# Linear attention into a feed-forward layer: reciprocals at the head of a period, quotients one period later

## The chip, the core and the metric

The kernel runs on one core of a Trainium2 chip. Its engines run side by side, each through its own instructions in order: TensorE (PE: matmuls; PEld: its weight loads), VectorE (DVE), ScalarE (ACT), GpSimd (POOL) and SyncE (SP), which here issues nearly all DMA transfers. The metric is the device time of one execution in microseconds (us), lower is better, given as the median of several runs.

## The reference

```python
def phi(x):
    proj = np.einsum('bhsd,df->bhsf', x, w_phi)
    proj = proj - np.max(np.abs(proj), axis=-1, keepdims=True)
    return np.concatenate([np.exp(proj), np.exp(-proj)], axis=-1)
q_p, k_p = phi(q), phi(k)                      # q, k, v: 8 x 8 x 576 x 64
kv = np.einsum('bhsf,bhsd->bhfd', k_p, v)
z = np.sum(k_p, axis=2)
num = np.einsum('bhsf,bhfd->bhsd', q_p, kv)
den = np.einsum('bhsf,bhf->bhs', q_p, z)[..., None] + 1e-06
x = (num / den)                                # rows put together: 4608 x 512
h = x @ w_in                                   # 512 x 2048, handed over in 8-byte floats
g = h - np.tanh(h)
out = g @ w_out                                # 2048 x 512, 8-byte floats
```

## The kernel before

**Attention.** Two heads form a unit; there are 32. `period(i)` is called for i = 0 to 32 and writes out by hand the order of everything; no scheduler reorders it. A period does one step for each of several units: `a` = unit i is projected in three rounds (`project`, line 214; each followed on VectorE by `less_max`: the maximum, line 224, and the subtraction, line 231, which frees the PSUM tile for the next round), and its key exponentials are taken; `c` = unit i-1 gets its K-V product (`kv`, line 274) and its transposed query side; `p` = unit i-2 gets numerator (`num`, line 319, copied to `d`) and denominator (`denom`, line 334).

For `r` = unit i-3 the denominator is copied to `dd` (line 349) and loaded, spread over 128 partitions, as `dn` (line 354). In the middle of the same period, behind the second round, comes `den_recip` (reciprocal `rn`, line 362, written to a row `rr` in DRAM, line 363) and `den_spread` (`rr` read back to 64 partitions for each head, `rb`, line 370). For `r2` = unit i-4, one period on, `den_mul` (line 375) multiplies `d` by `rb` on VectorE, and `x_store` (line 378) writes the result to DRAM (`xs`).

Each period also decodes one 128-row or 128-column block of w_in (even) or w_out (odd) from 8-byte floats: `dec_load` (lines 156 and 161, tile `raw`, two buffers), `dec_0` on ScalarE (line 168) and `dec_1` to `dec_3` on VectorE (lines 172 to 180). `split_w` splits decoded blocks into a rounded high part and a low part (POOL, line 97); fourteen of the 32 are split in attention, eighteen "late" ones in the first feed-forward group. `behind` (line 187) is a one-column copy that keeps POOL behind a VectorE instruction. The Q/K tile (576 KB, line 196) is loaded two periods ahead and V (320 KB, line 200) at the start of its own period, each into the buffer of two units before.

**Feed-forward.** Twelve groups of 384 rows, each in sixteen steps: `stage1` (lines 534 to 556: twelve matmuls, then ScalarE and VectorE work), `split_g` (`gh` on ScalarE, line 562; `gl` on POOL, line 563) and `stage2` (lines 569 to 572). Stage 2 trails stage 1 by two steps. Here a scheduler orders instructions, but those under `pin` keep program order. The last units' reciprocals and quotients (POOL's) and the late splits are put into the first group's steps.

Of the kernel before, what the change touches and what calls it, by code (L numbers as in the profile page):

```python
# [8 lines left out]
F32 = mybir.dt.float32  # L9
# [5 lines left out]
BF16 = mybir.dt.bfloat16  # L15
# [4 lines left out]
P = 128  # L20
# [12 lines left out]
def tile_linear_attention_moe(  # L33
# [10 lines left out]
    nc = tc.nc  # L44
    B, H, S, D = dims
# [11 lines left out]
    AHEAD = 7  # L57
    PC = 2 * S
    NCT = DM // P
    NF = DFF // P  # L60
# [61 lines left out]
    with ExitStack() as c1:  # L122
# [6 lines left out]
        ps_c = c1.enter_context(tc.tile_pool(name="ps_c", bufs=1, space=PSUM))  # L129
        ps_d = c1.enter_context(tc.tile_pool(name="ps_d", bufs=3, space=PSUM))  # L130

        zt = p1.tile([P, 256], BF16, name="zt")
        nc.gpsimd.memset(zt, 0.0)


        pw = ps_d.tile([P, 512], F32, tag="po", name="warm")

# [12 lines left out]
        def dec_load(n):  # L150
            u = Dec()
            u.nm = f"{'io'[n % 2]}{n // 2}"
            u.f, u.d = n // 2, (wi, wo)[n % 2]
            u.r = raw.tile([P, DM], U64, tag="raw", name=f"raw{u.nm}")
            if n % 2 == 0:
                nc.sync.dma_start(
                    u.r.rearrange("p (c f) -> p c f", f=P),
                    w_in[:, u.f * P : (u.f + 1) * P].rearrange("(c p) f -> p c f", p=P),
                )
            else:  # L160
                nc.sync.dma_start(u.r, w_out[u.f * P : (u.f + 1) * P, :])
            return u
# [7 lines left out]
        def dec_1(u):  # L170
            a = u.a
            nc.vector.tensor_scalar(f32(a), f32(a), CMIN, CMAX, ALU.max, ALU.min)
            nc.vector.tensor_scalar(a, a, 3, None, ALU.logical_shift_left)
# [4 lines left out]
        def dec_3(u):  # L178
            w = wpool.tile([P, DM], F32, tag="w", name=f"w{u.nm}")
            nc.vector.scalar_tensor_tensor(  # L180
                w.bitcast(U32), u.hi, 0x80000000, u.a, ALU.bitwise_and, ALU.bitwise_or
            )
            u.d[u.f] = w


        def behind(x):
            nc.gpsimd.tensor_copy(mark, f32(x[:, 0:1]))
# [10 lines left out]
        def load_v(u):  # L198
            u.v = p2.tile([P, 5, 2, D], F32, tag="v", name=f"v{u.i}")
            nc.sync.dma_start(u.v.rearrange("p j e d -> p (j e d)"), v5[u.i])  # L200
# [139 lines left out]
                        )  # L340

        def num_copy(u):
            u.d = tail.tile([P, S], F32, tag="d", name=f"d{u.i}", bufs=3)
            for c in range(2):
                nc.scalar.copy(u.d[:, c * CH : (c + 1) * CH], u.po[c][:, 0:CH])

        def denom_copy(u):
            u.dd = tail.tile([P, CH], F32, tag="dd", name=f"dd{u.i}", bufs=2)
            nc.scalar.add(u.dd, u.pd[:, 0:CH], 1e-6)

        def den_recip_load(u):
# [5 lines left out]
        def den_recip(u, pin=lambda ins: ins):  # L357
            dn = u.dn
            rr = dr.tile([2, S], F32, tag="rr", name=f"rr{u.i}")
            w = 2 * S // P  # L360
            rn = tail.tile([P, w], F32, tag="rn", name=f"rn{u.i}", bufs=4)
            pin(nc.vector.reciprocal(rn, dn))
            nc.sync.dma_start(rr.rearrange("a s -> (a s)").rearrange("(p c) -> p c", c=w), rn)
            u.rr, u.rn = rr, rn

        def den_spread(u):
            rr = u.rr
            rb = tail.tile([P, S], F32, tag="rb", name=f"rb{u.i}", bufs=2)
            for e in range(2):
                nc.sync.dma_start(rb[e * D : (e + 1) * D, :], rr[e : e + 1, :].broadcast_to([D, S]))  # L370
            u.rb = rb

        def den_mul(u, eng=nc.vector, pin=lambda ins: ins):
            x = u.rb
            pin(eng.tensor_tensor(x, u.d, x, ALU.mult))  # L375

        def x_store(u):
            nc.sync.dma_start(xs[u.b // 2][u.hp, :, (u.b % 2) * S : (u.b % 2 + 1) * S], u.rb)
# [16 lines left out]
        def unit(i):  # L395
            return units[i] if 0 <= i < NU else None
# [14 lines left out]
        lows = []  # L411

        def period(i):
            a, c, p, r, r2 = (unit(i - n) for n in range(5))
            w = dec[i - 2] if 2 <= i < NU + 2 else None
            last = i == NU
            if a:
                a.kp = kpb[i % 2]
                if i == 0:
                    warm(16)  # L420
                project(a, 0)
                less_max(a, 0)
            if r:
                denom_copy(r)
                den_recip_load(r)
            if 3 <= i <= NU:
                dec.append(dec_load(i - 1))
            if 1 <= i < NU:
                load_v(a)
            if p:  # L430
                ksum_copy(p)
            if w:
                if i == 2:
                    dec_0(w)
                dec_1(w)
            if r2:
                den_mul(r2)
                x_store(r2)
            n = i - 3
            if 0 <= n < 4 * AHEAD and n % 2 == 0:  # L440
                lows.extend(split_w(n // 2))
            if c:
                k_exp(c, 2)
                if w:
                    behind(r2.rb if r2 else w.a)
                kadd(c, (4,))
            if 0 <= n < 4 * AHEAD:
                lows.pop(0)()
            if p:
                num(p)  # L450
                num_copy(p)
            if last:
                for j in range(NCT):
                    x_split(xt[0], j)
            if i < 2:
                warm(8 + 26 * i)
            if a:
                project(a, 1, (ps_tr, "tr") if i == 0 else None)
                less_max(a, 1)
                k_exp(a, 0)  # L460
            if r:
                den_recip(r)
                den_spread(r)
            if w:
                dec_2(w)
                dec_3(w)
                behind(w.d[w.f])
            if c:
                kv(c)
                kv_copy(c)  # L470
            if last:
                ksum(c, ps_d, "po")
                ksum_copy(c)
            if a:
                k_exp(a, 1)
                kadd(a, (2, 3))
            if 2 <= i < NU:
                dec_0(dec[i - 1])
            if a:
                project(a, 2, (ps_d, "po") if i == 0 else None)  # L480
                less_max(a, 2)
            if i + 2 < NU:
                load(units[i + 2])
            if c:
                turn(([(p, "s")] if p else []) + [(c, "k")] + ([(c, "s")] if last else []))
                q_side(c)
            if p:
                denom(p)
            if c and not last:
                ksum(c)  # L490
            if last:
                num(c)
                num_copy(c)
                dec_0(dec[i - 1])
                denom_copy(p)
                den_recip_load(p)
                w = dec[NU - 1]
                dec_1(w)
                dec_2(w)
                dec_3(w)  # L500
                denom(c)
                denom_copy(c)
                den_recip_load(c)
            if i == NU - 6:
                xt[0] = x_tiles(0)
            if 0 <= i - (NU - 6) < NCT:
                x_load(0, xt[0], i - (NU - 6))
# [6 lines left out]
    with ExitStack() as c2:  # L514
# [73 lines left out]
        for i in range(len(steps) + 2):  # L588
            if i < len(steps):
                g, f = steps[i]  # L590
                if f == 0:
                    po[g] = [ps_o.tile([P, DM], F32, tag="o", name=f"po{g}_{t}") for t in range(G)]
                gs[i] = stage1(g, f, *xt[g][:2])
                if g + 1 < NG:
                    if f == 0:
                        xt[g + 1] = x_tiles(g + 1)
                    if f % 3 == 0 and f < 3 * NCT:
                        x_load(g + 1, xt[g + 1], f // 3)
                    if f % 3 == 2 and f < 3 * NCT:
                        x_split(xt[g + 1], f // 3, pin)  # L600
            if 1 <= i <= len(steps):
                g, f = steps[i - 1]
                gg[i - 1] = split_g(g, f, gs.pop(i - 1), G)
            if 1 <= i <= 2:
                den_recip(units[i - 3], pin)
                den_spread(units[i - 3])
            if 2 <= i <= 4:
                den_mul(units[i - 5], nc.gpsimd, pin)
                x_store(units[i - 5])
            while late and late[0] <= 2 * AHEAD + i * NL // (NF - 1):  # L610
                split_w(late.pop(0), pin)[0]()
            if i >= 2:
                g, f = steps[i - 2]
                stage2(po[g], f, *gg.pop(i - 2), G)
                if f == NF - 1:
                    store(g * G, po.pop(g), G)
# [55 lines left out]
```

## Time and profile before

| | |
|---|---|
| median of 3 runs | 1168.69 us (1167.58 to 1170.34) |
| the profiled execution | 1172.38 us, its span 1170.6 |
| busy, share of the span | PE 97%, VectorE 74%, ScalarE 71%, POOL 36% |
| attention | about the first 356 us |
| DMA share, attention from 33.65 to 344.96 us | 0.61, 190 GB/s |
| DMA share, 450 us to the end | 0.07, 22 GB/s |

A row of the timeline gives start, duration, engine, line, operation, output and input; in brackets, how long the engine idled before it and what ended that. `SPq` rows are DMA issues on SyncE's queue, not transfers. "To landing" is from an issue to its data in place. In the list of waits stand total, number and longest.

### The profile page before, as it was taken

The page shows a single profiled execution, that of the slowest core. Times are in us where ns is not written, and L with a number is a line of the kernel's source. Part 1 is how long each engine was busy: PE and PEld are TensorE (multiplying, and loading weights), DVE is VectorE, ACT ScalarE, POOL GpSimd, SP SyncE. Part 2 cuts the span into 40 slices and gives each one's busy share as a digit, 9 for nine tenths or more (in the row PEclk, how much of TensorE's full clock was granted, in tenths as well). Part 3 has the DMA queues.
Part 4 walks back from the last instruction along what each step waited for, and adds up shares of the span by engine and source line. Part 5 has one row for each costly group of instructions (what it writes and reads, how often), then busy time and mean ns, then how long its engine had stood idle before and what let it go on. Part 6 is the DMA issues. An engine that isn't in the chain of part 4 may idle for free.

```text
span 1170.6 us, 21022 instructions
## 1 busy us (share of the span) xinstructions
PE 1137.5 (97%) x7578; PEld 951.9 (81%) x7578; DVE 863.3 (74%) x1429; ACT 833.4 (71%) x1908; POOL 417.3 (36%) x441
## 2 busy tenths in 40 slices
PE   8998999999899999999999999999999999999998
PEld 6666666666568889999999999999999999999996
DVE  5788688788777877677777767777777767777665
ACT  4876877788678766676766667676676667676665
POOL 3565466465545742222222222222222222222222
PEclk9999999999999999999999999999999999999999
DMA  4556565666652000010000000010101001000000
GB/s 153 158 185 199 174 195 195 210 194 187 203 170 81 31 29 21 8 41 14 34 21 34 15 21 28 15 41 14 35 15 34 21 8 41 14 28 1 28 1 28
DMA packets 51177, 85.61 MB, mean 73 GB/s; under 512 B 13313, under 2 KB 28033, under 8 KB 51073
## 3 DMA queue, kind: packets, MB, share of 16 engines
q1 hardware_dynamic: 50912, 84.20, 22.8%
q8 instruction: 60, 0.98, 0.4%
q14 instruction: 45, 0.36, 0.1%
q10 hardware_dynamic: 160, 0.07, 0.0%
HBM read 65.08 MB, written 19.02 MB: 72 GB/s over the span
## 4 chain that ended last, share of the span: by engine, by line
PE 78%; DMA 11%; DVE 5%; ACT 2%; issue 2%; POOL 1%; SPq 1%; DVEq 0%; ACTq 0%; POOLq 0%
PE ph L534 33%; PE po L572 11%; PE po L570 11%; PE po L569 11%; DMA rb<-rr 5%; DMA rr<-rn 3%; PE pp L214 3%; PE po L319 2%; DVE m L224 2%; DMA rawo<-in_moe_w_out 2%; PE pd L334 2%; PE pc L274 1%; PE ptt L241 1%; DVE t L231 1%; DVE rb L375 1%
## 5 line engine op out<-in xcount | busy, mean ns | idle before, releaser
L563 POOL TENSOR_TENSOR gl<-s,gh 128x384 fp32r<-128x384 f32 x192 | 196.0, 1021 | 568.7 <-ACT gh L562 567.5
L541 ACT ACTIVATE y<-ph 128x384 f32<-128x384 f32 x192 | 94.5, 492 | 238.1 <-PE ph L534 238.1
L534 PE MATMUL ph<-xh,wli 128*128 128x384 f32 x768 | 259.1, 337 | 0.8 <-POOL wli L97 0.8
L534 PE MATMUL ph<-xh,whi 128*128 128x384 f32 x768 | 258.7, 337 | 0.0
L534 PE MATMUL ph<-xl,whi 128*128 128x384 f32 x768 | 257.9, 336 | 0.0
L550 DVE SCALAR_TENSOR_TENSOR s<-s,y 128x384 f32<-128x384 f32 x192 | 110.9, 577 | 174.3 <-ACT s L543 174.2
L569 PE MATMUL po<-who,gh 128*128 128x512 f32 x576 | 227.1, 394 | 1.6 <-ACT gh L562 1.6
L570 PE MATMUL po<-wlo,gh 128*128 128x512 f32 x576 | 226.8, 394 | 0.0
L572 PE MATMUL po<-who,gl 128*128 128x512 f32 x576 | 164.3, 393 | 1.3 <-POOL gl L563 1.3
L534 PEld LDWEIGHTS ph<-xh,whi 128*128 128x128 f32 x768 | 144.3, 188 | 8.9 <-issue 0.5
L534 PEld LDWEIGHTS ph<-xl,whi 128*128 128x128 f32 x768 | 144.1, 188 | 8.2
L534 PEld LDWEIGHTS ph<-xh,wli 128*128 128x128 f32 x768 | 144.0, 188 | 1.2 <-POOL wli L97 1.2
L556 DVE COPY_PREDICATED s<-mk,th 128x384 f32<-128x384 uint32 x176 | 123.7, 703 | 18.9 <-DVE th L555 0.9
L572 PEld LDWEIGHTS po<-who,gl 128*128 128x128 f32 x576 | 107.9, 188 | 27.6 <-POOL gl L563 2.9
L224 DVE TENSOR_REDUCE m<-pp 128x4 f32<-128x512 f32 (+3 forms) x98 | 91.8, 939 | 49.9 <-PE pp L214 48.7
L283 POOL TENSOR_TENSOR ss<-ss,kp 128x512 f32<-128x512 f32 x96 | 122.7, 1278 | 9.4 <-ACT kp L268 4.4
L569 PEld LDWEIGHTS po<-who,gh 128*128 128x128 f32 x576 | 107.8, 187 | 20.2 <-ACT gh L562 3.3
L570 PEld LDWEIGHTS po<-wlo,gh 128*128 128x128 f32 x576 | 108.2, 188 | 16.3
L268 ACT ACTIVATE kp<-t 128x256 f32<-128x256 f32 (+2 forms) x256 | 108.4, 481 | 17.6 <-DVE t L231 16.4
L543 ACT ACTIVATE s<-y,bias_t 128x384 f32<-128x384 f32 x192 | 118.4, 617 | 3.3 <-POOL gl L563 3.3
L549 ACT ACTIVATE mk<-y,bias_t 128x384 f32<-128x384 f32 x192 | 117.7, 613 | 0.5 <-DVE s L556 0.5
L214 PEld LDWEIGHTS pp<-wph,qk 64*128 64x128 f32 x1152 | 74.0, 190 | 49.6 <-issue 19.0
(353 smaller groups left out, 1744.6 us busy)
## 6 DMA issues: line engine op xcount, KB each, us to landing
qk<-in_qkT SPq DMA_DIRECT2D x31, 576.0 KB, 4.9
v<-in_v SPq DMA_DIRECT2D x32, 320.0 KB, 5.3
rb<-rr SPq DMA_DIRECT2D x64, 144.0 KB, 3.4
xs<-rb SPq DMA_DIRECT2D x32, 288.0 KB, 3.9
x<-xs SPq DMA_DIRECT2D x48, 192.0 KB, 2.4
out<-o SPq DMA_DIRECT2D x36, 256.0 KB, 2.3
rawi<-in_moe_w_in SPq DMA_DIRECT2D x16, 512.0 KB
rawo<-in_moe_w_out SPq DMA_DIRECT2D x16, 512.0 KB
```

Source lines behind the costliest of these rows:

```text
L214: nc.tensor.matmul(heads[e][:, o * F : (o + 1) * F], u.qk[hs, j * P : (j + 1) * P], wph[hs, :], start=True, stop=True)
L224: nc.vector.tensor_reduce(m[:, e], x, AX.X, ALU.max, apply_absolute_value=True)
L283: nc.gpsimd.tensor_tensor(u.ss, u.ss, u.kp[:, :, j], ALU.add)
L534: nc.tensor.matmul(h, wt[:, c * P : (c + 1) * P], x[:, c, 0:N], start=(i == 0), stop=(i == 3 * NCT - 1))
L543: nc.scalar.activation(s1, y, AF.Square, bias=bias_t[:, 0:1])
L549: nc.scalar.activation(mk, y, AF.Relu, bias=bias_t[:, 2:3])
L550: nc.vector.scalar_tensor_tensor(s1, s1, PC1, y, ALU.add, ALU.mult)
L556: nc.vector.copy_predicated(gs, mk.bitcast(U32), hh)
L563: pin(nc.gpsimd.tensor_tensor(gl, gs, f32(gh), ALU.subtract))
L569: nc.tensor.matmul(po[t], a, wo[f][0], start=(f == 0), stop=False)
L570: nc.tensor.matmul(po[t], a, wo[f][1], start=False, stop=False)
L572: nc.tensor.matmul(po[t], gl[:, t * P : (t + 1) * P], wo[f][0], start=False, stop=(f == NF - 1))
```

## The change

- The reciprocal of a unit moves from the middle of period u+3 to the head of period u+4, ahead of the first round. Its quotient and store move from period u+4 to u+5 (`r3`), at the same place in the period. The spread follows the store of the unit before it.
- `d` has four buffers in place of three; `dd` one in place of two.
- V is loaded one period earlier, behind the spread; its buffer's last reader is the K-V product of the same period. A weight block is loaded behind `dec_3`, the last reader of its buffer, and so about half a period earlier.
- At the end three units are left for reciprocals (steps 5, 7, 9 of the first group; before, two in steps 1 and 2) and four for quotients (6, 8, 10, 12; before, three in 2 to 4). The late splits run in steps 2 to 14 (0 to 15 before).
- The matmuls that keep TensorE busy at the start read the identity in place of a zero tile, which is no longer written.

```diff
-        zt = p1.tile([P, 256], BF16, name="zt")
-        nc.gpsimd.memset(zt, 0.0)
+        zt = ident.bitcast(BF16)
...
-            u.d = tail.tile([P, S], F32, tag="d", name=f"d{u.i}", bufs=3)
+            u.d = tail.tile([P, S], F32, tag="d", name=f"d{u.i}", bufs=4)
...
-            u.dd = tail.tile([P, CH], F32, tag="dd", name=f"dd{u.i}", bufs=2)
+            u.dd = tail.tile([P, CH], F32, tag="dd", name=f"dd{u.i}", bufs=1)
...
-            a, c, p, r, r2 = (unit(i - n) for n in range(5))
+            a, c, p, r, r2, r3 = (unit(i - n) for n in range(6))
...
+            if r2:
+                den_recip(r2)
             if a:
...
-            if 3 <= i <= NU:
-                dec.append(dec_load(i - 1))
-            if 1 <= i < NU:
-                load_v(a)
...
+            if r3:
+                den_mul(r3)
+                x_store(r3)
             if r2:
-                den_mul(r2)
-                x_store(r2)
+                den_spread(r2)
+            if i + 1 < NU:
+                load_v(units[i + 1])
...
-                    behind(r2.rb if r2 else w.a)
+                    behind(r3.rb if r3 else w.a)
...
-            if r:
-                den_recip(r)
-                den_spread(r)
             if w:
                 dec_2(w)
                 dec_3(w)
+                if i < NU:
+                    dec.append(dec_load(i))
...
-            if 1 <= i <= 2:
-                den_recip(units[i - 3], pin)
-                den_spread(units[i - 3])
-            if 2 <= i <= 4:
-                den_mul(units[i - 5], nc.gpsimd, pin)
-                x_store(units[i - 5])
-            while late and late[0] <= 2 * AHEAD + i * NL // (NF - 1):
+            if i in (5, 7, 9):
+                u = units[NU - 3 + (i - 5) // 2]
+                den_recip(u, pin)
+                den_spread(u)
+            if i in (6, 8, 10, 12):
+                u = units[NU - 4 + (i - 6) // 2]
+                den_mul(u, nc.gpsimd, pin)
+                x_store(u)
+            while late and late[0] < 2 * AHEAD + (i - 1) * NL / (NF - 3):
                 split_w(late.pop(0), pin)[0]()
```

In the rows below the number behind a name tells tiles of one kind apart. VectorE in a middle period, from the quotient on, before:

```order
L375 TENSOR_TENSOR rb_1394<-d_1226,rb_1394 128x576
L224 TENSOR_REDUCE m_1_1525<-pp_1_1518 128x6
L231 TENSOR_TENSOR t_1_1527<-pp_1_1518,m_1_1525 128x768
L362 RECIPROCAL rn_1534<-dn_1488 128x9
L176 SCALAR_TENSOR_TENSOR dec_ai_1420<-rawi_1344,dec_ai_1420 128x512
L180 SCALAR_TENSOR_TENSOR wi_1541<-rawi_1344,dec_ai_1420 128x512
L224 TENSOR_REDUCE m_2_1574<-pp_2_1565 128x8
L231 TENSOR_TENSOR t_2_1576<-pp_2_1565,m_2_1574 128x1024
L224 TENSOR_REDUCE m_0_1625<-pp_0_1620 128x4
```

And with the change (its lines are numbered two lower):

```order
L373 TENSOR_TENSOR rb_1347<-d_1081,rb_1347 128x576
L222 TENSOR_REDUCE m_1_1523<-pp_1_1516 128x6
L229 TENSOR_TENSOR t_1_1525<-pp_1_1516,m_1_1523 128x768
L174 SCALAR_TENSOR_TENSOR dec_ai_1413<-rawi_1245,dec_ai_1413 128x512
L178 SCALAR_TENSOR_TENSOR wi_1532<-rawi_1245,dec_ai_1413 128x512
L222 TENSOR_REDUCE m_2_1567<-pp_2_1558 128x8
L229 TENSOR_TENSOR t_2_1569<-pp_2_1558,m_2_1567 128x1024
L360 RECIPROCAL rn_1614<-dn_1485 128x9
L222 TENSOR_REDUCE m_0_1622<-pp_0_1617 128x4
```

The reciprocal has moved from behind the second round's subtraction to behind the third's; the quotient keeps its place. SyncE's DMA issues of one period, before, from the denominator's load on:

```order
L354 DMA dn_1342<-dd_1340 128x1x9
L156 DMA rawi_1344<-in_moe_w_in 128x4x128
L200 DMA v_1346<-in_v 128x640
L378 DMA xs_75<-rb_1248 128x576
L363 DMA rr_1390<-rn_1391 128x9
L370 DMA rb_1394<-rr_1390 64x576 x2
L196 DMA qk_1435<-in_qkT 128x1152
```

And with the change, from the reciprocal's row on:

```order
L361 DMA rr_1324<-rn_1325 128x9
L352 DMA dn_1339<-dd_1337 128x1x9
L376 DMA xs_75<-rb_1204 128x576
L368 DMA rb_1347<-rr_1324 64x576 x2
L198 DMA v_1350<-in_v 128x640
L159 DMA rawo_1391<-in_moe_w_out 128x512
L194 DMA qk_1428<-in_qkT 128x1152
```

The same eight issues: the reciprocal's row now goes first, the spread behind the store, and V, weight block and Q/K load stand in a row behind the spread, just ahead of the next period's row. POOL in the first group, from its first `gl` to the one of step 3, before and with the change:

```order
L563 TENSOR_TENSOR gl_0_4893<-s_0_4845,gh_0_4892 128x384
L97 TENSOR_TENSOR wlo_4904<-wo_2554,who_4903 128x512
L563 TENSOR_TENSOR gl_1_4937<-s_1_4880,gh_1_4936 128x384
L375 TENSOR_TENSOR rb_4699<-d_4555,rb_4699 128x576
L97 TENSOR_TENSOR wli_4950<-wi_2697,whi_4949 128x512
L563 TENSOR_TENSOR gl_2_4992<-s_2_4922,gh_2_4991 128x384
```

```order
L562 TENSOR_TENSOR gl_1_4911<-s_1_4865,gh_1_4910 128x384
L97 TENSOR_TENSOR wli_4915<-wi_2399,whi_4914 128x512
L97 TENSOR_TENSOR wlo_4919<-wo_2545,who_4918 128x512
L562 TENSOR_TENSOR gl_2_4961<-s_2_4896,gh_2_4960 128x384
L97 TENSOR_TENSOR wli_4965<-wi_2688,whi_4964 128x512
L562 TENSOR_TENSOR gl_3_5005<-s_3_4946,gh_3_5004 128x384
```

The quotient ahead of `gl_2` is gone from there, and two low parts stand in one step.

## The prediction

> **What bounds the kernel now.** I read first the busy time by stretch, cut where a period's numerator matmuls (line 319) start, which is instant 0 of a period below.
>
> ```profile
> 33.65:344.96 311.31, 289.88 (x3155) 195.83 (x3153) 248.91 (x348) 241.49 (x624) 174.49 (x202) 0.99 0.61 190
> 355.80:450.00 94.20, 91.29 (x457) 81.01 (x454) 74.72 (x131) 69.47 (x149) 50.38 (x42) 1.00 0.12 38
> ...
> 107.34:120.79 13.45, 10.73 (x112) 7.17 (x110) 8.63 (x12) 8.78 (x25) 6.85 (x8) 0.94 0.51 162
> 163.14:173.04 9.90, 9.90 (x111) 6.72 (x110) 8.55 (x12) 8.44 (x23) 6.08 (x8) 1.00 0.64 200
> 204.45:215.40 10.95, 10.03 (x111) 6.76 (x109) 8.62 (x12) 8.60 (x23) 5.42 (x8) 1.00 0.60 188
> 215.40:227.35 11.95, 9.97 (x112) 6.76 (x110) 8.62 (x12) 8.64 (x23) 6.01 (x8) 1.00 0.65 196
> ```
>
> Columns: stretch, length, busy PE, PEld, DVE, ACT, POOL, clock, DMA share, GB/s. TensorE is the bound wherever nothing disturbs it: an undisturbed attention period takes 9.90 us with PE busy all of it. The 29 stretches from 33.65 to 344.96 took 311.31 us. At 9.90 each, the last one 0.65 shorter because no next first round stands in it, they would take 286.45. So 24.9 us are lost in attention: 21.4 of PE idle (311.31 less 289.88), the rest matmuls that run slower behind a stall (clock 0.94 around the longest). The first feed-forward group loses 2.9 (94.20 less 91.29). Next, what ends the waits, over 33 to 345 us:
>
> ```profile
> DVE rb L375 <- DMA rb<-rr: 19.3, 18, 2.2
> ACT dec_ao L168 <- DMA rawo<-in_moe_w_out: 7.4, 7, 2.7
> ACT dec_ai L168 <- DMA rawi<-in_moe_w_in: 2.7, 3, 1.7
> ```
>
> VectorE waits 18 times, 19.3 us, for the spread reciprocals ahead of the quotient; ScalarE 10 times, 10.1 us, for a weight block to decode. How such a wait reaches PE:
>
> ```profile
> 207.95 0.76 DVE L375 TENSOR_TENSOR rb<-d,rb 128x576 f32<-128x576 f32 x1 [1.17 <-DMA rb<-rr]
> 210.71 1.16 PE L214 MATMUL pp<-wph,qk 64*128 64x128 f32 x16 [0.92 <-DVE rn L362]
> 219.95 0.76 DVE L375 TENSOR_TENSOR rb<-d,rb 128x576 f32<-128x576 f32 x1 [2.22 <-DMA rb<-rr]
> ```
>
> Behind the quotient on VectorE stand the second round's maximum and subtraction, and PE's third round needs their PSUM tile. A wait of 1.17 made its period 10.95 (1.05 over), 2.22 made 11.95 (2.05 over): each costs its length less some 0.17 of slack.
>
> **The change, part by part.** First the reciprocal's chain, before:
>
> ```profile
> 158.19 0.20 DVE L362 RECIPROCAL rn<-dn 128x9 f32<-128x9 f32 x1
> 160.98 1.22 DVE L231 TENSOR_TENSOR t<-pp,m 128x1024 f32<-128x1024 f32 x1
> 163.26 0.69 DVE L224 TENSOR_REDUCE m<-pp 128x4 f32<-128x512 f32 x1 [1.06 <-PE pp L214]
> 165.39 0.75 DVE L375 TENSOR_TENSOR rb<-d,rb 128x576 f32<-128x576 f32 x1
> ...
> 158.41 0.33 SPq L363 DMA_DIRECT2D rr<-rn  x1
> 161.37 1.10 SPq L370 DMA_DIRECT2D rb<-rr  x2
> 162.57 0.54 SPq L196 DMA_DIRECT2D qk<-in_qkT  x1
> 164.34 0.42 SPq L156 DMA_DIRECT2D rawi<-in_moe_w_in  x1
> 164.81 0.99 SPq L200 DMA_DIRECT2D v<-in_v  x1
> 166.16 0.33 SPq L378 DMA_DIRECT2D xs<-rb  x1
> ...
> DMA to landing us min/median/max: 1.4/2.8/4.4
> DMA to landing us min/median/max: 2.1/3.4/6.4
> ```
>
> The last two rows are landing times of rr and of rb. The row to DRAM goes out 5.2 into the period (158.41 less 153.24, where the period that ended at 163.14 began), the spread 8.1 in, and the quotient wants it at 12.15 (165.39 less 153.24): 6.98 us. Two issues of 0.33 and 1.10 plus the medians 2.8 and 3.4 are 7.6. It is late in most periods, by about what the waits show.
>
> Afterwards the reciprocal stands behind the third round's subtraction, whose end (160.98 and 1.22, 162.20) is 0.94 before the next period's instant 0. Its 0.20 on VectorE falls inside the 1.06 that VectorE idles there for PE: nothing; with that cover gone 29 times 0.20, 5.8. rr goes out near -0.7 and lands near 2.1 (median) to 3.7 (longest). The spread now also stands behind the quotient and its store on SyncE: the store went out 3.0 in (166.16 less 163.14), so the spread goes at 3.4 to 4.0 and lands by 7.9 on medians (1.10 and 3.4 more). The quotient wants it in the next period at 12.15. Slack of 4, where 0.6 was missing; even the longest landing, 6.4, ends at 11.5. So all 18 waits go: 19.3 less 18 times 0.17, **-16.2**.
>
> The weight block goes out now behind its buffer's last reader, and so half a period earlier than its turn was:
>
> ```profile
> 168.88 0.69 DVE L180 SCALAR_TENSOR_TENSOR wo<-rawo,dec_ao 128x512 uint32<-128x512 uint32 x1
> 169.94 0.69 ACT L168 ACTIVATE dec_ai<-rawi 128x512 f32<-128x512 f32 x1
> 109.26 7.76 DMA rawo<-in_moe_w_out
> ```
>
> Issue to use was 164.34 to 169.94, 5.6 us; afterwards from 169.57 (the end of the 168.88 row) to the same use a period later, 9.9 plus 0.4: 10.3. The longest that the chain of waits shows is 7.76. These waits carry the rest of the loss, 24.9 less 16.2: **-8.7**, the slow clock included. If they stay, that is the price.
>
> The V load takes one period more of lead, and a wait: its buffer's reader is the current period's K-V product, which ends 5.3 in:
>
> ```profile
> 156.20 2.38 PE L274 MATMUL pc<-kp,v 128*64 128x256 f32 x20
> ```
>
> Behind it on SyncE stand the weight block and the Q/K load, both due 10 us or more later, and the next rr. One denominator buffer in place of two makes a copy wait for the load of 9.9 us before: nothing, but for the last two copies, which follow at once:
>
> ```profile
> 355.59 0.80 ACT L349 ACTIVATE dd<-pd 128x288 f32<-128x288 f32 x2
> 358.18 0.49 ACT L541 ACTIVATE y<-ph 128x384 f32<-128x384 f32 x1 [1.79 <-PE ph L534]
> 312.80 4.17 DMA dn<-dd
> ```
>
> The last copy now stands behind y. It waits until the load behind the first copy (its end, 355.59 and half of 0.80, is 356.0) lands: 1.4 (rr's shortest, a transfer of the same size) to 4.17 later, 357.4 to 360.2, while y is done at 358.67. Cost 0 to 1.5 on the first group's chain; a weight rounding that stood in step 0 leaves that chain, so I take 0. The fourth numerator buffer only lets the quotient wait. The zero tile's removal touches nothing: the start waits for the projection weights.
>
> In the first feed-forward group low parts and quotients are respaced on POOL.
>
> ```profile
> 368.62 1.61 DVE L116 TENSOR_TENSOR xl<-x,xh 128x384 fp32r<-128x384 f32 x1
> L92 DVE CAST who<-wo x9: 364/413/1212, 365.5 to 426.7; 128x512 fp32r<-128x512 f32 x9
> 369.77 1.61 POOL L97 TENSOR_TENSOR wli<-wi,whi 128x512 fp32r<-128x512 f32 x1
> 378.71 1.44 POOL L375 TENSOR_TENSOR rb<-d,rb 128x576 f32<-128x576 f32 x1 [1.60 <-DMA rb<-rr]
> 382.73 0.97 PE L572 MATMUL po<-who,gl 128*128 128x512 f32 x3 [1.10 <-POOL gl L563]
> 420.39 0.45 PE L534 MATMUL ph<-xh,wli 128*128 128x384 f32 x1 [0.79 <-POOL wli L97]
> ```
>
> PE's 1.10 follows a quotient that made POOL wait 1.60 for its spread: spread and quotient now stand three steps apart, gone. The 0.79 for the last low part of w_in goes too, it now comes two steps ahead of its reader. Against that, step 2 now holds two low parts ahead of its own gl, the second behind a rounding (364 to 1212 ns) that VectorE does only after its split, which ends at 370.23: it starts at 370.6 to 371.4, where the POOL instruction just ahead of that gl started at 369.77: 0.8 to 1.7 later. Bounds: -2.9 (all gone) to +2 (four more such steps with two); I take **-1.2**.
>
> For a wait that no row shows I leave **+1.0**, between 0 and 8.7. Sum: -16.2 - 8.7 - 1.2 + 1.0 = -25.1. The profiled execution took 1172.4 (span 1170.6), so 1147.3; it lies 3.7 above the median 1168.69. If the 3.7 are longer stalls of that execution, the runs land at 1147.3 too; if a fixed cost of recording, at 1143.6. Between them: **1145.5**.
>
> **The rivals.** *The ring (slower).*
>
> ```profile
> qk<-in_qkT SPq DMA_DIRECT2D x31, 576.0 KB, 4.9
> v<-in_v SPq DMA_DIRECT2D x32, 320.0 KB, 5.3
> rawi<-in_moe_w_in SPq DMA_DIRECT2D x16, 512.0 KB
> ```
>
> V, weight block and Q/K now leave as one burst of 1408 KB from 5.4 on, and rr, 4.5 KB, is issued behind it, as is dn. SyncE takes its issues in order: rr 0.33, its landing L, spread 1.10, V 0.99, block 0.42, Q/K 0.54, then the next rr. That loop needs 3.4 + L, and above L = 6.5 it, not PE, sets the period. For it: rr had no Q/K load just ahead of it before. Against: at 200 GB/s and a share of 0.64 the engines move 312 GB/s when full, so 1442 kB take 4.6 us, done near 10 to 11.7, when rr has just been issued: L near 3 to 4. At L = 7.76, the longest landing seen, a period is 11.1, 1.24 over, 29 times 36, less 24.9 gained: 1180. The Trainium skill ("DMA: Bandwidth & Descriptors", Queues, rings and completion order) speaks for this rival: on each engine a queue's descriptors are consumed in ring order, so a small transfer waits out the large ones ahead. By that alone rr lands after Q/K; the trace's rr landings of 1.4 to 4.4 do not contradict it.
>
> *Half the gain.* The blocks now queue behind V and the spread; if ScalarE still waits as before, 8.7 stays: 1154. For it: landings up to 7.76 with less ahead. Against: 2.5 us of slack over that.
>
> *No change.* The stalls are not the transfers' but move to another wait of the same period, as VectorE's slack of 0.3 at the third round would allow. Against: nine of the 29 stretches are clean (9.89 to 9.94) with the same instructions in them. 1168.7.
>
> **How the numbers follow.** Forecast 0.66 (1141 to 1150), half the gain 0.20 (1150 to 1160), no change 0.04, slower 0.10. Anything within 0.2% is what this measurement cannot tell from no change. Faster 0.86, same 0.04, slower 0.10. The range, 1140 to 1158, takes in the first group's lower bound (1.7 more) at the fixed-cost end and the block waits at the other.
>
> **What would show it.** Right: periods of 9.90 to 9.95 by stretch, no VectorE wait on rb, no ScalarE wait on raw blocks, SyncE waiting for rr near 3 us, PE idle in the first group under 2.9. Wrong: rr landings above 6, SyncE waiting for rr into the spread of the period behind, or a new releaser ahead of PE's third round.

## The result, and the profile after

| | before | after |
|---|---|---|
| median | 1169.51 us (1167.58 to 1170.67, 4 runs) | 1142.68 us (1142.49 to 1142.94, 4 runs) |
| the profiled execution | 1172.38, span 1170.6 | 1142.88, span 1141.1 |

Time after over time before is 0.9772, with a 95% interval of 0.9755 to 0.9789: 26.8 us faster. The forecast was 1145.5 in a range of 1140 to 1158.

The spans of the two profiled executions differ by 29.5 us. Where that went is read by stretch. The changed kernel, in the columns of the prediction's first fence: the start, the 29 attention stretches between the same two numerator matmuls, and the first feed-forward stretch:

```profile
0.00:31.66 31.66, 28.74 (x288) 21.21 (x288) 20.23 (x29) 18.28 (x44) 14.39 (x22) 1.00 0.52 168
31.66:318.11 286.45, 286.45 (x3155) 194.50 (x3154) 250.25 (x347) 237.32 (x623) 175.35 (x202) 1.00 0.64 205
329.00:423.10 94.10, 92.97 (x466) 83.20 (x465) 78.64 (x135) 70.87 (x153) 52.15 (x43) 1.00 0.13 42
```

The 29 stretches took 286.45 with TensorE busy for all of it at a clock of 1.00, against 311.31 before: 24.86 of the 29.5. That is the length the prediction gave for 29 undisturbed periods. They begin 1.98 earlier (31.66 for 33.65). The rest, 29.5 less 24.86 less 1.98, is 2.7 and comes behind them; 1.8 of it is PE idle in the first group's stretch, 1.1 (94.10 less 92.97) where 2.9 stood; where the other 0.9 lies is not followed up here.

The chain of work that ended last says the same in one line, with no transfer left in it:

```profile
PE 96%; DVE 2%; POOL 1%; ACT 1%; issue 1%; DVEq 0%; POOLq 0%
```

The waits of the changed kernel from 30 to 320 us (total, number, longest). These are VectorE's and ScalarE's largest; none of their waits is for a transfer, and of SyncE's only the last row is:

```profile
DVE m L222 <- PE pp L212: 28.7, 31, 1.1
ACT kvt L290 <- PE pc L272: 39.7, 29, 1.4
SPq L368 <- DMA rr<-rn: 12.2, 13, 2.2
```

The last row, in the same stretch of the kernel before:

```profile
SPq L370 <- DMA rr<-rn: 74.9, 26, 5.1
```

This is the pair of rows on which everything below turns: SyncE stood 74.9 us, in 26 periods, with the spread at the head of its queue, waiting for the row of reciprocals to land in DRAM. Now it stands 12.2.

What stood behind it shows in the kernel before at the longest stall of attention. SyncE's queue, and the decode that then ran late on ScalarE:

```profile
102.61 0.33 SPq L363 DMA_DIRECT2D rr<-rn  x1
106.75 1.10 SPq L370 DMA_DIRECT2D rb<-rr  x2
107.95 0.53 SPq L196 DMA_DIRECT2D qk<-in_qkT  x1
...
109.26 0.42 SPq L161 DMA_DIRECT2D rawo<-in_moe_w_out  x1
...
117.04 0.67 ACT L168 ACTIVATE dec_ao<-rawo 128x512 f32<-128x512 f32 x1 [2.66 <-DMA rawo<-in_moe_w_out]
```

The spread goes out 4.14 us behind the row (106.75 less 102.61). Behind it four transfers leave in one bunch, the 512 KB block 1.31 us after the 576 KB Q/K load, and this block is the one that took 7.76 us to land. In the changed kernel the same queue over one period reads:

```profile
169.47 0.33 SPq L361 DMA_DIRECT2D rr<-rn  x1
170.79 0.59 SPq L352 DMA_DIRECT2D dn<-dd  x1
173.28 0.32 SPq L376 DMA_DIRECT2D xs<-rb  x1
173.93 1.53 SPq L368 DMA_DIRECT2D rb<-rr  x2
175.63 0.46 SPq L198 DMA_DIRECT2D v<-in_v  x1
176.73 0.34 SPq L159 DMA_DIRECT2D rawo<-in_moe_w_out  x1
177.16 0.38 SPq L194 DMA_DIRECT2D qk<-in_qkT  x1
179.37 0.33 SPq L361 DMA_DIRECT2D rr<-rn  x1
```

The row's landing falls mostly into the time in which SyncE stands anyway, first for the denominators' copy and then for the quotient to be stored (33.7 and 47.6 us of waits from 30 to 320 us). The large loads leave behind the small transfers, and no engine waits for any of them.

### The profile page after: what moved, and what is told of

The parts are those of the page before. It is cut to its first block, busy times and chain, and to the rows that moved or that the text cites. A ratio compares the mean times of both kernels' runs of the same rounds, so it can differ in the third digit from the quotient of the medians.

```text
span 1141.1 us, 21052 instructions
## 1 busy us (share of the span) xinstructions
PE 1131.7 (99%) x7578; PEld 950.3 (83%) x7578; DVE 866.3 (76%) x1428; ACT 829.3 (73%) x1908; POOL 418.9 (37%) x441
## 4 chain that ended last, share of the span: by engine, by line
PE 96%; DVE 2%; POOL 1%; ACT 1%; issue 1%; DVEq 0%; POOLq 0%
PE ph L533 34%; PE po L568 11%; PE po L571 11%; PE po L569 11%; PE pp L212 7%; PE pc L272 6%; PE po L317 6%; PE pd L332 3%; PE ptt L239 2%; PE pk L286 1%; PE ptr L245 1%; POOL gl L562 0%; PE warm L138 0%; DVE xl L116 0%; POOL wli L97 0%
## 5 line engine op out<-in xcount | busy, mean ns | idle before, releaser
L551 DVE SCALAR_TENSOR_TENSOR s<-s,s 128x384 f32<-128x384 f32 x176 | 98.2, 558 | 17.6 <-ACT mk L548 0.5
```

Source lines behind the costliest of these rows:

```text
L551: nc.vector.scalar_tensor_tensor(gs, s2, PC2, s1, ALU.add, ALU.mult)
```

## The experiments

The theories named in the expectations are those held when each run was written down; several of them fell. In each heading stands which kernel the edit starts from. A time of one execution is called one run; the kernel before ranged from 1162.5 to 1176.6 over all runs made beside these, so single times of kernels that still wait differ by some us for no reason of their edit.

### The change, with the V and block loads where they were

```diff
             if r:
                 denom_copy(r)
                 den_recip_load(r)
+            if 3 <= i <= NU:
+                dec.append(dec_load(i - 1))
+            if 1 <= i < NU:
+                load_v(a)
...
-            if i + 1 < NU:
-                load_v(units[i + 1])
...
-                if i < NU:
-                    dec.append(dec_load(i))
```

> The change with its two loads put back: V and the weight block leave at the start of the period again, 5.7 us ahead of the block's use. Theory (the loss of 24.9 in attention is two separable waits, 16.2 on the spread reciprocals and 8.7 on the weight block): no VectorE wait on rb, ScalarE waits on raw come back, 2 to 9 us in all, periods up to 11, 1144.5 to 1151.5. Rival (the block was late only because the spread and the Q/K load were pushed behind each other by the quotient's waits): no wait on raw either, all periods 9.90, 1142.5 to 1143.5.

Measured: 1142.94 us (1142.53 to 1143.08, 4 runs), 0.9787 of before (0.9756 to 0.9818): the change's own time. The only wait for a transfer that is left on ScalarE or VectorE from 30 to 320 us:

```profile
ACT dec_ai L166 <- DMA rawi<-in_moe_w_in: 0.3, 1, 0.3
```

So the prediction's reason for the 8.7 us of block waits falls: with the block leaving as late as before, they are gone too, to 0.3. The theory that the waits of VectorE and of ScalarE are two separate debts is wrong, and the rival's forecast right. The rival's reason, that the quotient's waits pushed the spread and the Q/K load together, is tested further down and does not hold either.

### The kernel before, with those load moves alone

The edit is the reverse of the one above, made on the kernel before.

> The kernel before with only the two loads moved (V one period earlier behind the store, the block behind the last reader of its buffer); reciprocal and quotient as before. V now stands just ahead of the reciprocal's row in SyncE's order, the block behind the spread, some 6 us ahead of its use. Theory: the waits on rb stay and become more frequent, since V's 320 KB go out just ahead of rr: 18 to 29 waits, 16 to 45 us; the waits on raw shrink to under 6; 1158 to 1185. Rival (the loads caused the late spreads by standing ahead of them in the ring early in the period): waits on rb under 8 us, 1145 to 1152.

Measured: 1169.26 (1166.61 to 1173.54, 10 runs), 1.0004 of before (0.9984 to 1.0024): nothing gained. ScalarE's waits for blocks are gone, as meant, but VectorE's waits (30 to 320 us) now come for two transfers:

```profile
DVE rn L362 <- DMA dn<-dd: 17.8, 21, 2.0
DVE rb L375 <- DMA rb<-rr: 10.5, 12, 2.0
```

The time fell where the theory had it, the waits did not: it had all of them on the spread. With the block let out ahead of Q/K, the 4.5 KB denominators now stand last in the bunch, and the reciprocal is late. The debt moved from one transfer to another.

### The change, with reciprocal and spread back in the middle of the period

```diff
-            if r2:
-                den_recip(r2)
...
-            if r2:
-                den_spread(r2)
...
+            if r and not last:
+                den_recip(r)
+                den_spread(r)
             if w:
                 dec_2(w)
```

> The change with the reciprocal back in the middle of its old period, its spread behind it, and only the quotient one period later; loads as in the change, so the block stands behind the spread, some 6 us ahead of its use. Theory (what matters is the time from reciprocal to quotient, not that the reciprocal is at the head): no wait on rb; a few waits on raw, 0 to 5 us; 1142.5 to 1148. Rival (the reciprocal must be out of the period's middle, since its row then stands behind V and the block in the ring and SyncE waits there with the loads behind it): waits on raw in most periods or periods over 10.2, 1152 to 1165.

The quotient still comes a period later and the loads still leave early. Measured: 1169.22 (1165.3 to 1175.15, 10 runs), 0.9996 of before (0.9971 to 1.0022). The whole gain is gone; the theory, for which the quotient's extra period was what counted, is wrong. The rival came nearer, but the median lies above its 1152 to 1165 too, and it had the blocks late, for which no wait is left here. SyncE's queue and the reciprocal on VectorE:

```profile
168.76 1.10 SPq L368 DMA_DIRECT2D rb<-rr  x2
169.96 0.53 SPq L159 DMA_DIRECT2D rawo<-in_moe_w_out  x1
170.59 0.38 SPq L194 DMA_DIRECT2D qk<-in_qkT  x1
171.06 0.59 SPq L352 DMA_DIRECT2D dn<-dd  x1
...
176.53 0.21 DVE L360 RECIPROCAL rn<-dn 128x9 f32<-128x9 f32 x1 [1.43 <-DMA dn<-dd]
```

The same three transfers leave in a bunch once the spread is out, and the last of them, 4.5 KB behind 1088, makes VectorE wait: 30.0 us in 26 waits from 30 to 320 us.

### The same, with the loads where they were too

The edit is the one above plus that of the first experiment.

> The change with the reciprocal and its spread back in the middle of their old period and both loads back at the start of theirs; only the quotient comes a period later. Unlike in the kernel with the moved loads, the denominator's load no longer stands behind the block and Q/K. Theory A (SyncE's wait for rr in the period's middle holds the Q/K load back, which then stands just ahead of the weight block in the ring; that, not the quotient's waits, made the block late): no wait on rb, waits on raw stay, 3 to 12 us, 1145 to 1155. Theory B (everything followed from the quotient's waits): no waits, 1142.4 to 1144.

Measured: 1164.86 (1161.39 to 1171.95, 10 runs), 0.997 of before (0.9952 to 0.9989): 3.5 us or so, where 13 to 23 were expected. The theory is right in kind, since no wait for the spread is left, and wrong in size (it had 3 to 12 us of waits for blocks): these, 9 of together 9.1 us in the kernel before from 30 to 320 us, are 21 of 19.1 there, and the reciprocal waits as well.

```profile
ACT dec_ao L166 <- DMA rawo<-in_moe_w_out: 10.2, 11, 1.9
ACT dec_ai L166 <- DMA rawi<-in_moe_w_in: 8.9, 10, 1.9
DVE rn L360 <- DMA dn<-dd: 7.9, 10, 1.6
```

A quotient that comes later only passes the lateness on, to the block that is now the tightest. SyncE's wait for the row is longer than before, 97.1 us in 27 waits, so the blocks were not late because of the quotient's waits: with these gone, the blocks are later still.

### The change, with the quotient in the period of its reciprocal

```diff
-            if r3:
-                den_mul(r3)
-                x_store(r3)
             if r2:
                 den_spread(r2)
+                den_mul(r2)
+                x_store(r2)
...
-            if i in (6, 8, 10, 12):
+            if i in (8, 10, 12):
```

> The change with the quotient in the same period as the reciprocal that now stands at its head. Theory: row, spread and quotient follow each other within the period, 0.33 + 2 to 4.3 + 1.1 + 3.1 from reciprocal to quotient where VectorE has 2.95 of other work: a wait of 3.5 to 5.5 in each of 28 periods, 1240 to 1300. If the reciprocal's place were what matters: no more than the change, 1143 to 1150.

Measured: one run, 1273.36, inside what the theory gave. The reciprocal is early, and SyncE hardly waits for its row (12.8 us), but the quotient stands right behind the spread's issue:

```profile
DVE rb L373 <- DMA rb<-rr: 60.1, 20, 4.7
```

The time came out in the range partly by luck. The waits are 3.0 us a period, less than the 3.5 to 5.5 expected; the 29 stretches take 409.79 us, and TensorE is busy for 332.60 of them, 46 more than with the change, at a granted clock of 0.87.

So neither half of the change works without the other: the early reciprocal needs the quotient's extra period, and the quotient's extra period gains nothing while SyncE waits for the row in mid-period.

### The kernel before, with one issue moved

```diff
                 den_recip(r)
-                den_spread(r)
...
                 load(units[i + 2])
+            if r:
+                den_spread(r)
```

> The kernel before with one thing changed: the spread is issued behind the Q/K load, so that SyncE's wait for rr no longer holds that load back and the weight block no longer stands just behind it. Theory A: ScalarE's waits on raw (10.1 us before) fall under 2 us; the spread itself comes behind 576 KB and is later, waits on rb 25 to 70 us, 1175 to 1215. Theory B (the block is late because the quotient's waits upset the order): more waits on rb, so as many or more on raw, 10 us or more.

Only the order of two issues on SyncE changes: the Q/K load no longer stands behind the wait for the row. Measured: one run, 1152.47, against 1165.6 to 1173.21 (15 runs) of the kernel before on that chip. Its queue, its waits from 30 to 320 us and its 29 stretches:

```profile
179.67 0.33 SPq L363 DMA_DIRECT2D rr<-rn  x1
180.96 0.33 SPq L196 DMA_DIRECT2D qk<-in_qkT  x1
182.85 1.12 SPq L370 DMA_DIRECT2D rb<-rr  x2
...
185.60 0.42 SPq L161 DMA_DIRECT2D rawo<-in_moe_w_out  x1
```
```profile
SPq L370 <- DMA rr<-rn: 30.3, 24, 2.0
...
DVE rb L375 <- DMA rb<-rr: 6.4, 11, 1.8
```
```profile
33.37:324.57 291.20, 287.24 (x3155) 195.05 (x3153) 248.89 (x348) 238.65 (x623) 174.82 (x202) 1.00 0.65 202
```

No block is late: it leaves 4.64 us behind Q/K (185.60 less 180.96), not 1.31. That part of the theory holds. Its other part, that the spread would then wait longer for the row and the quotient with it (25 to 70 us), does not: quotients wait 6.4 us in 11 waits, against 16.7 in 16 in the same stretch before, and SyncE's own wait for the row fell as well, to 30.3. Attention loses 4.75 us (291.20 less 286.45) where the profiled execution of before lost 24.86: moving one issue recovers four fifths of what the whole change does there. This is the run that shows where the loss came from. It is a single execution, but 13.1 us below the fastest of the 15 beside it.

### How large a margin the new order has: 576 KB more in each period

```diff
...
             if i + 2 < NU:
                 load(units[i + 2])
+                for _ in range(1 if i >= 3 else 0):
+                    nc.sync.dma_start(spare[i % 2], qkT[units[i + 2].i])
```

The extra transfer copies Q/K into rows of DRAM that nothing reads.

> The change with one more transfer of 576 KB in each period (Q/K of the unit once more, to a spare row in DRAM that nobody reads), issued behind the Q/K load and so just ahead of the reciprocal's row. Theory: rr lands some 1.9 later (576 KB at 312 GB/s), near 6 us, still under the 6.5 at which SyncE's loop would set the period; the quotient keeps its slack; periods 9.90 to 9.95, 1142.5 to 1144. Rival (the ring): rr above 6.5 us, SyncE's loop of 3.4 and rr's landing sets the period: 10.2 or more, 1151 or more.

Measured: one run, 1171.45. SyncE's queue over one of its periods, the wait for the row from 30 to 320 us, and one stretch:

```profile
159.08 0.51 SPq L362 DMA_DIRECT2D rr<-rn  x1
...
166.94 1.11 SPq L369 DMA_DIRECT2D rb<-rr  x2
...
169.25 0.38 SPq L195 DMA_DIRECT2D qk<-in_qkT  x1
169.68 0.54 SPq L485 DMA_DIRECT2D spare<-in_qkT  x1
170.31 0.53 SPq L362 DMA_DIRECT2D rr<-rn  x1
```
```profile
SPq L369 <- DMA rr<-rn: 136.1, 26, 6.3
```
```profile
155.75:167.13 11.38, 9.97 (x111) 6.76 (x109) 8.73 (x12) 8.81 (x24) 6.07 (x8) 1.00 0.72 233
```

This is the prediction's slower rival at work, in a kernel where it has been given its condition. From the row's issue to the spread's are 7.86 us, from there to the next row 3.37: a loop of 11.23 on SyncE, and the period in which the spread goes out takes 11.38 with TensorE busy for 9.97. The prediction had 3.4 + L, with the row's landing L, above L = 6.5. The DMA engines are busy for 0.72 of the stretch only: the bytes don't set the period, the small row that waits behind them does.

TensorE feels this late. The first seven of the 29 stretches still take 9.90, while the rows fall behind: those at 40.35 and 104.05 are six periods apart and 4.3 us more than six times 9.90. That is about the quotient's slack of 4 us. From then on VectorE waits for the spread again, 27.2 us in 19 waits from 30 to 320 us, and the 29 stretches lose 28.8 (315.23 less 286.45), the whole difference to the change.

### And 288 KB more

The same with half of each row's columns.

> The change with one more transfer of 288 KB in each period, half of the one that raised rr's landing from 4.3 to 7.9 us. By the same slope rr lands after 6.1, SyncE's loop is 3.4 + 6.1 = 9.5, under the 9.90: periods of 9.90 to 10.0, 1142.5 to 1146. If the loop was not what bound there, but a step once any transfer is added: periods over 10.5, 1158 or more.

Measured: one run, 1142.88, the change's time. One row and its spread:

```profile
188.98 0.33 SPq L362 DMA_DIRECT2D rr<-rn  x1
...
195.29 1.10 SPq L369 DMA_DIRECT2D rb<-rr  x2
```

6.31 us, just under 6.5, and nothing lost: the 29 stretches take 286.45 again. This is close to the limit. In attention the time from the row's issue to the spread's runs up to 6.69, and by the row at 300.77 the rows had fallen behind by up to 2.9 us, which the quotient's slack took in. The margin lies between 288 and 576 KB a period, and the two runs agree with the point of 6.5 worked out before the result, without fixing it more closely.

### Two such transfers

```diff
-                for _ in range(1 if i >= 3 else 0):
+                for _ in range(2 if i >= 3 else 0):
```

> As before, with two such transfers in each period. Theory: the DMA engines are full (3136 KB in a period are 10.3 us at 312 GB/s), rr lands near 8, SyncE's loop is 11.4: periods of 10.3 to 11.5, 1153 to 1185, with waits of VectorE on rb or of SyncE on rr into V's turn. If the ring order costs nothing: the full engines alone set 10.3, 1153.

Measured: one run, 1283.22, above what either theory gave, and not to be read as the price of bytes. The two transfers of a period write the same row of DRAM, so SyncE held the second until the first had landed, a wait put in by this edit:

```profile
SPq L485 <- DMA spare<-in_qkT: 122.9, 19, 7.6
```

This run settles nothing on the margin.

### The change, with the late splits' steps as before

```diff
-            while late and late[0] < 2 * AHEAD + (i - 1) * NL / (NF - 3):
+            while late and late[0] <= 2 * AHEAD + i * NL // (NF - 1):
```

> The change with the late splits spaced as before (steps 0 to 15 of the first feed-forward group). Theory: PE's idle before the last low part of w_in and before the gh behind it (0.8 each) comes back, so 1143.5 to 1144.5. Rival A (the whole 2.6 that the feed-forward part gained came from the spacing of the splits): 1145 to 1145.5. Rival B (it came from the quotients' new steps): within 0.3 of the change, 1142.4 to 1143.0.

Measured: 1144.21 (1144.1 to 1144.76, 4 runs), 0.98 of before (0.9774 to 0.9826): the theory's 1143.5 to 1144.5. TensorE's waits from 326 to 480 us, for this kernel:

```profile
PE ph L533 <- POOL wli L97: 1.1, 2, 0.8
PE po L568 <- ACT gh L561: 1.0, 2, 0.8
```

and for the change:

```profile
PE ph L533 <- POOL wli L97: 0.7, 1, 0.7
PE po L571 <- POOL gl L562: 0.4, 1, 0.4
```

Spacing the splits is worth 1.5 us (1144.21 less 1142.68); of the 2.7 behind attention some 1.2 are left, which may be the quotients' new steps; no run takes these back alone.

### The change, with the last quotient two steps later

```diff
-            if i in (6, 8, 10, 12):
-                u = units[NU - 4 + (i - 6) // 2]
+            if i in (6, 8, 10, 14):
+                u = units[NU - 4 + (6, 8, 10, 14).index(i)]
```

> The change with the last unit's quotient in step 14 of the first feed-forward group instead of 12, out of the way of the low part of w_in's block 14, for which PE waits 0.69 us with the change. Theory: that wait goes, 1141.8 to 1142.3. Otherwise another low part takes its place: 1142.4 to 1143.

Measured: 1142.2 (1141.93 to 1143.77, 5 runs), 0.9774 of before (0.975 to 0.9799). The 0.7 us wait for the last low part of w_in is gone from TensorE's waits. The median is 0.5 us under the change's, but these runs were not made beside it and their own times lie 1.8 us apart: no difference that these runs separate.

### The kernel before, with the identity in place of the zero tile

```diff
-        zt = p1.tile([P, 256], BF16, name="zt")
-        nc.gpsimd.memset(zt, 0.0)
+        zt = ident.bitcast(BF16)
```

> The kernel before with only the zero tile replaced by the identity. The first numerator matmul started at 23.74 us before and 21.76 with the change. Theory (the 2 us are the moment at which the second half of the projection weights lands, and vary from run to run): between 21.7 and 23.8, the same in kernels of either kind; attention's waits as before, 1167 to 1171. Rival (identity matmuls keep TensorE's clock up where zeros don't, or spare a wait): 21.8 in this kernel, 23.7 in every kernel with the zero tile.

Measured: one run, 1169.41, where the kernel before took 1162.5 in the one run beside it: no gain that shows through the stalls. SyncE waits for the row as in the kernel before, 79.3 us in 27 waits. The first numerator matmul, which ends the start, stood at 23.74 in the profile of before and at 21.76 in that of the change. Here it stands at 22.10. With the identity it lies between 21.28 and 22.10 in every profile of this study. With the zero tile there are three profiles: 23.74, 23.46 in the kernel with one issue moved, and, in the kernel with the load moves alone,

```profile
21.58 2.16 PE L319 MATMUL po<-qe,kv0k 128*64 128x288 f32 x16
```

So the zero tile does not hold the start back each time; whether it does so in some executions, these runs leave open. The two late starts have one thing in common that the profiles show: TensorE's matmuls up to there run longer. The eight warm-up matmuls behind the first projection round take 1.89 us in both, and 1.05 to 1.67 in all other profiles; the 36 projection matmuls that follow take 2.83 in the profile of before, 2.28 with the change. The granted clock reads 1.00 in both, and TensorE's only wait for the projection weights is one of 0.15 in one of them, so neither theory nor rival is borne out.

## Why the prediction was right, and where its steps were not

- **The bound, and what the stalls cost: right.** 29 undisturbed periods were to take 286.45 and took 286.45; the loss found there, 24.9, came back as 24.86.
- **VectorE's waits, -16.2: the chain right, the price not a term of its own.** The row's chain: "rr goes out near -0.7", "the spread goes at 3.4 to 4.0". In the changed kernel's period that begins with

```profile
170.25 0.95 PE L317 MATMUL po<-qe,kv14s 128*64 128x288 f32 x6
```

  the row went out at 169.47, -0.8, and the spread at 173.93, 3.7 in. No wait on the spread is left. The fourth experiment, though, removes all these waits too and gains 3.5 us: the spread's waits and the block's are one debt, and 16.2 plus 8.7 met the loss because the second term was taken as what the first leaves of it. One sign named for a right forecast did not show: SyncE was to wait for the row near 3 us, and waits 12.2 us in 13 waits, 2.2 at the longest, since it stands for the quotient's store first. Two readings were off and did no harm: the landing row 2.1/3.4/6.4 takes in the quotient's stores, and the spread alone has 2.8/3.4/4.7; and the slack of the two waits shown is 0.12 and 0.17, not 0.17 in both.
- **"The weight block goes out now behind its buffer's last reader, and so half a period earlier", -8.7: the sum right, the reason wrong.** This is the step that failed. Undoing the move costs 0.3 us of waits, and making it alone gains nothing. The block was late because SyncE takes its issues in order and stood up to 5.1 us at the spread; Q/K was held there and came out 1.3 us ahead of the block. The prediction had the row for it, the 7.76 landing, and the queue's order in the fence beside it, but priced the spread's wait by the quotient alone and not by what stood behind it on SyncE. The Trainium skill ("DMA: Bandwidth & Descriptors", Anatomy of one DMA — SWDGE (gpsimd) path) says that the DMA engines wait on no semaphore and that each wait is served on the issuing sequencer before the transfer is handed over; the Q/K load at 107.95, behind a spread held to 106.75, agrees.
- **The ring, 0.10: rightly last, with its formula right and one term low.** 3.4 + L with its point of 6.5 agrees with the runs on both sides (6.31: 9.90; 7.86: 11.38). But "L near 3 to 4" was low: the median landing of the row went from 2.8 to 4.3, longest 5.4, so 1.1 of margin was left at the longest, where the sum had 2.5 or more. The mis-sized step is the end of the burst, put at 10 to 11.7 into the period: Q/K goes out at 177.16, 6.9 in, and takes 6.0 (its median), so it is in place 12.9 in, at 183.2. The row behind it, from 179.37 with its median of 4.3, lands at 183.7. The rule of the Trainium skill quoted there ("DMA: Bandwidth & Descriptors", Queues, rings and completion order), that on each engine a ring is consumed in order, agrees with these medians. In the first experiment, where V and the block are not in that bunch, the row's median is 2.3. Landings (shortest, median, longest) of the changed kernel's row, and behind it those of the first experiment's:

```profile
DMA to landing us min/median/max: 1.4/4.3/5.4
```
```profile
DMA to landing us min/median/max: 1.4/2.3/4.4
```

- **The first group, -1.2: right in sign, too small.** 1.8 came in the group's stretch, 2.7 with all that lies behind attention. Of the two waits priced, the 1.10 behind the quotient went. The 0.79 for a low part of w_in was to go as well and did not: 0.7 is left, and it goes only when the last quotient is moved further. In its place a wait of 0.8 for `gh` went that the sum had not named. The only wait on a `gl` that is left is the one of 0.4 above.
- **The left-over wait, +1.0: none came.** The margin of 4 at the quotient held.
- **One denominator buffer, 0: right.** The last copy stood behind y and waited for nothing:

```profile
331.35 0.49 ACT L540 ACTIVATE y<-ph 128x384 f32<-128x384 f32 x1 [2.21 <-PE ph L533]
331.74 0.40 ACT L347 ACTIVATE dd<-pd 128x288 f32<-128x288 f32 x1
```

- **The start, 0: it came out 2.0 earlier in the profiles.** Where the time lies is said above; the cause is open.
- **From profile to median.** Of the profiled execution 1147.3 was forecast and 1142.9 measured: 4.4 apart: 1.0 for the wait, 1.5 for the group and what lies behind it, 2.0 for the start, rounded. The 3.7 us by which the profiled execution of before lay above its median were not a fixed cost of recording, since 0.2 is left of them; the runs of the kernel before reach to 1176.6, so it lay inside their own spread. That 1145.5 missed the median by 2.8 and not by more is luck in part: half of those 3.7 had been taken off as a hedge, while the sum itself missed by 4.4.

## What to carry to other kernels

An issue that waits for another transfer to land holds everything behind it on its queue: price that wait by what is queued behind it, down to which transfers then leave in one bunch and which of them is needed first, and not only by the one that it delays. The wait that the profile names (here a weight block on ScalarE) can be two steps from its cause, so try the order of two issues before moving the load that is named. Where a small transfer closes a loop through such a queue, work out the landing time from which the loop sets the period, and add bytes until it does: that gives the margin.

## What the runs showed of the hardware that was not expected

- A 4.5 KB transfer took longer to land the more had been issued just ahead of it: 2.3 us with the 576 KB Q/K load alone there, 4.3 with V and a block (832 KB) ahead of that, 6.3 from its issue to the spread's with another 288 KB, 7.9 with another 576 KB, while the DMA engines were busy for 0.64 to 0.72 of the time. Not all of this is the amount: in the periods shown the row followed Q/K by 2.21 us with the change (177.16 to 179.37) and by 1.06 with 576 KB more (169.25 to 170.31), and these runs do not part the two.
- The kernels that wait for transfers have the wider spread of times: 1162.5 to 1176.6 (before, all its runs), 1166.61 to 1173.54 (the load moves alone), 1165.3 to 1175.15 and 1161.39 to 1171.95 (the two with only the quotient later). The change, the one with its loads put back and the one with its splits put back, four runs each, stay within 0.7 us, and the one with the last quotient later, five runs, within 1.84. That the waits make the spread is not shown by this.
